# One row of the output projection moved from the last load of a decode kernel to its first

## The chip, the cores and the metric

The kernel runs on one core of one Trainium2 chip. The metric is device time in microseconds of one execution. In the profile PE is TensorE (PEld its weight loads), DVE is VectorE, ACT is ScalarE, POOL is GpSimd and SP is SyncE.

## The reference

One token passes through a layer with two parallel branches, attention over a sliding window of cached keys and values, and a small MLP:

```
xn  = layernorm(x)                                # x: 1 x 1024
q   = xn @ wq                                     # wq: 1024 x 4096, 32 heads of 128
k,v = last W = 4096 positions of the caches       # 4 kv heads, each for 8 query heads
p   = softmax(q k^T / sqrt(128));  o = p v
A   = o @ wo                                      # wo: 4096 x 1024
B   = gelu(layernorm(xn) @ w1 + b1) @ w2 + b2     # w1: 1024 x 3584, w2: 3584 x 1024
out = x + A + B                                   # 1 x 1024, bf16
```

All inputs are bf16. Nearly all bytes are read once: wq and wo 8 MB each, w1 and w2 7 MB each, 4 MB of K and 4 MB of V.

## The kernel before, in words

Four large buffers in SBUF, `slot0` to `slot3`, each 128 partitions by 16384 bf16, are reused in turn. Every large load goes through SP's queue, one after another, in the order in which SP issues it. A load into a slot that is still being read is issued only when the readers are done, so SP waits at these places.

The order of loads is: wq's first row and K's four heads (before a barrier of all engines at L203), then wq's other rows in three loads, b1 and b2, w1 in two loads, V, w2 in three loads, and wo in seven. "Row" c of wq, wo, w1 and w2 is what one matmul step takes: a tile of 128 partitions, one weight row on each partition; the view is `"(p c) n -> p c n"`. wo has 32 such rows (`CWO`), each 128 x 1024 bf16, 256 KB, of 2 KB per partition. Rows 0 to 15 go into `slot0` in two loads of eight rows. Rows 16 to 31 go into `slot2` in five loads, cut at

```
cuts = [0, 8, 12, 14, 15, 16]
```

so that the last two loads hold one row each, 30 and 31. A load is the unit that is waited for: each has a semaphore of its own, and `wo_row(c)` gives the tile and the key of the load that row c came with.

The work is written as a list of operations with the names that they read and write. The class `Plan` works out from it which operation waits for which; each engine then carries out its own in the order of the list.

VectorE transposes K (L334, four steps) and copies it into order (L343, shared with ScalarE, L339). TensorE multiplies by wq meanwhile. Scores, softmax, V and the MLP's first half follow. VectorE sums 21 of w2's 28 rows, each scaled by its activation, in f32 (`run[0]`, `run[1]`; L479 and L482) and adds the two sums in L518. TensorE does the other seven (`PE_ROWS`) and wo's rows 0 to 23 (`NB` is 24) into `sc_ps` as `bulk`. VectorE then adds `bulk` to `run[0]` (L550, in two halves).

The end of the kernel is the loop over wo's rows 24 to 31. Each row is four matmuls into the two banks of `acc2` (`acc_a` 288 columns wide, `acc_b` 224), with the two halves of the output at partitions 0 and 32. After row 27 eight f32 matmuls (L233 in the profile) fold `run[0]` into the same accumulators. L227 is the helper `mm` in which all the single-row matmuls are recorded, L219 the helper `ldw` for their weights, and L213 the helper `dma`. VectorE (L569) and ScalarE (L570) cast the two banks to bf16, and SP and ScalarE store the halves.

The loads ahead of the barrier are issued at L194 (K) and L199 (wq's first row, and x on ScalarE's queue). The plan learns of them by entries that issue nothing and only name the semaphore, such as

```
plan.add("sp", lambda: None, (), ("wq0",), wq_sem)
```

Of the kernel before, what the change touches and what calls it, by code (L numbers as in the profile page):

```python
# [8 lines left out]
BF16 = mybir.dt.bfloat16  # L9
# [123 lines left out]
def kernel(  # L133
# [14 lines left out]
    nc = tc.nc  # L148
    P = 128
    D = A_x.shape[-1]  # L150
    Hkv = A_k_cache.shape[1]
    Sk = A_k_cache.shape[2]
    Dh = A_k_cache.shape[3]
    NQ = A_wq.shape[1]
    Hq = NQ // Dh
# [8 lines left out]
    CWO = NQ // P  # L164
    NA = 288
    NB = 24
# [7 lines left out]
    def sb(name, shape, dt):  # L174
        return nc.alloc_sbuf_tensor(name, shape, dt).ap()

    def ps(name, shape):
        return nc.alloc_psum_tensor(name, shape, FP32).ap()

    slot = [sb(f"slot{i}", [P, 16384], BF16) for i in range(4)]  # L180
    kT = sb("kT", [P, 4, 4, W // 4], BF16)
    acc2 = ps("acc2", [P, 2, 512])
# [4 lines left out]
    x_flat = A_x.rearrange("a b d -> (a b d)")  # L187
    k_sb, kt_scr = slot[0], slot[3]
    k_sem = [nc.alloc_semaphore(f"k{g}") for g in range(Hkv)]
    wq_v = A_wq.rearrange("(p c) n -> p c n", p=P)  # L190
    wq_sem = nc.alloc_semaphore("wq0")

    def load_k(g):
        return nc.sync.dma_start(out=k_sb[g:P - Hkv + g + 1:Hkv, :],  # L194
                                 in_=A_k_cache[0, g, Sk - W:Sk, :].rearrange("(r c) d -> r (c d)", r=P // Hkv))

    x32 = sb("x32", [Hq, Hq], BF16)
    x_sem = nc.alloc_semaphore("x32")
    for i, sem in [(nc.sync.dma_start(out=slot[1][:, 0:NQ], in_=wq_v[:, 0, :]), wq_sem)] + [(load_k(g), k_sem[g]) for g in range(Hkv)] + [(nc.scalar.dma_start(out=x32, in_=x_flat.rearrange("(a j) -> a j", a=Hq)), x_sem)]:  # L199
        i.then_inc(sem, 16)  # L200
        tc.no_tile_sem_insts.add(i.ins.name)
    tc.close()
# [2 lines left out]
    plan = Plan(nc)  # L205
    pe, dve, act, pool, sp = nc.tensor, nc.vector, nc.scalar, nc.gpsimd, nc.sync

    def op(eng, fn, r=(), w=()):
        plan.add(eng, fn, r, w)

    def dma(eng, out_ap, in_ap, r=(), w=(), over=()):
        q = plan.engines[eng]
        plan.add(eng, lambda: q.dma_start(out=out_ap, in_=in_ap), r, w, True, over)  # L213

    def ldw(w_ap, pos, r):
        def go():
            with nc.discard():
                i = pe.ldweights(w_ap, tile_position=pos).ins
            return pe.add_instruction(mybir.InstLdweights(  # L219
                name=nc.get_next_instruction_name(), engine=i.engine, tile_size=(P, 32), tile_position=pos, ins=i.ins, outs=i.outs))  # L220
        op("pe", go, r, ())

    def mm(out_ap, w_ap, x_ap, start, stop, pos, r, w):
        def go():
            with nc.discard():
                i = pe.matmul(out_ap, lhsT=w_ap, rhs=x_ap, start=start, stop=stop, tile_position=pos).ins
            return pe.add_instruction(mybir.InstMatmult(  # L227
                name=nc.get_next_instruction_name(), engine=i.engine, start_tensor_calc=start, stop_tensor_calc=stop,
                tile_size=i.tile_size, tile_position=i.tile_position, ins=i.ins, outs=i.outs, ldweights=False))
        op("pe", go, r, w)  # L230

    def mm32(out_ap, w_ap, x_ap, start, stop, r, w, pos=None):
        op("pe", lambda: pe.matmul(out_ap, lhsT=w_ap, rhs=x_ap, start=start, stop=stop, tile_position=pos), r, w)  # L233

    plan.add("sp", lambda: None, (), ("wq0",), wq_sem)
    for g in range(Hkv):
        plan.add("sp", lambda: None, (), (f"k{g}",), k_sem[g])
# [1 line left out]

    w1_v = B_w1.rearrange("(p c) n -> p c n", p=P)  # L240
    w2_v = B_w2.rearrange("(p c) n -> p c n", p=P)
    wo_v = A_wo.rearrange("(p c) n -> p c n", p=P)
    wq_t = [slot[1 + i].rearrange("p (r n) -> p r n", r=4) for i in range(2)]
    wq_cuts = ((0, 1, 2), (0, 2, 4), (1, 0, 4))
    for i, a, b in wq_cuts:
# [91 lines left out]
    for s0, s1 in ((0, 1), (1, 2), (2, 4)):  # L337
        for (R, Cd) in pairs[:ACT_PAIRS]:
            op("act", lambda s0=s0, s1=s1, R=R, Cd=Cd: act.copy(out=kT[32 * Cd:32 * Cd + 32, R, s0:s1, :].rearrange("p s (c j) -> p (s c) j", j=32),  # L339
                                                                in_=T3[32 * R:32 * R + 32, 32 * s0:32 * s1, Cd, :]), [f"scr{s}" for s in range(s0, s1)], (f"kTa{R}{Cd}{s0}",))  # L340
    kt_keys = [f"kTa{R}{Cd}{s}" for (R, Cd) in pairs[:ACT_PAIRS] for s in range(3)]
    for n, (R, Cd) in enumerate(pairs[ACT_PAIRS:]):
        op("dve", lambda R=R, Cd=Cd: dve.tensor_copy(out=kT[32 * Cd:32 * Cd + 32, R, :, :].rearrange("p s (c j) -> p (s c) j", j=32),  # L343
                                                     in_=T3[32 * R:32 * R + 32, :, Cd, :]), [f"scr{s}" for s in range(NS)], (f"kTd{R}{Cd}",))
# [32 lines left out]
    for c in (2, 3):  # L377
        for t in range(4):
            ldw(xw[:, 96 + P * c:97 + P * c], (0, 32 * t), ("xw",))
        for b in range(2):  # L380
            for t in range(4):
                j = 2 * (3 - t) + b
# [121 lines left out]
    wo_t = [slot[s].rearrange("p (r n) -> p r n", r=16) for s in (0, 2)]  # L504
    for a in (0, 8):
        dma("sp", wo_t[0][:, a:a + 8, :], wo_v[:, a:a + 8, :], (), (f"wo0{a}",), ("slot0",))
    cuts = [0, 8, 12, 14, 15, 16]
    for a, b in zip(cuts[:-1], cuts[1:]):
        dma("sp", wo_t[1][:, a:b, :], wo_v[:, 16 + a:16 + b, :], (), (f"wo1{a}",), ("slot2",))
    o_m = sb("o_m", [Hq, Hkv, Dh], FP32)  # L510
# [26 lines left out]
    o8 = sb("o8", [P, 32], BF16)  # L537
# [2 lines left out]
    bulk_rows(PE_ROWS, w2_row, hcol, "hT", first=True)  # L540

    def wo_row(c):
        i, r = divmod(c, 16)
        return wo_t[i][:, r, :], f"wo0{r // 8 * 8}" if i == 0 else f"wo1{max(a for a in cuts if a <= r)}"

    ocol = lambda c: o8[:, c:c + 1]
    bulk_rows(list(range(16)), wo_row, ocol, "o8")
    bulk_rows(list(range(16, NB)), wo_row, ocol, "o8", last=True, groups=2)
    for half in range(2):
        op("dve", lambda half=half: dve.tensor_tensor(out=run[0][0:33, 512 * half:512 * half + 512], in0=bulk[:, half, :],  # L550
                                                      in1=run[0][0:33, 512 * half:512 * half + 512], op=ALU.add), ("bulk", "run0"), (f"sum{half}",))
    acc_a, acc_b = acc2[:, 0, 0:NA], acc2[:, 1, 0:512 - NA]
    parts = [(acc_a, 0, NA, "acc_a"), (acc_b, NA, 512, "acc_b")]
    for c in range(NB, CWO):
        wap, key = wo_row(c)
        for half in range(2):
            ldw(o8[:, c:c + 1], (0, 32 * half), ("o8",))
        for acc, a, b, akey in parts:
            for half in range(2):
                pr, h0 = 32 * half, 512 * half  # L560
                mm(acc[pr:pr + 1, :], o8[:, c:c + 1], wap[:, h0 + a:h0 + b], c == NB, c == CWO - 1, (0, pr), (key,), (akey, "acc2"))
        if c == NB + 3:
            for acc, a, b, akey in parts:
                for half in range(2):
                    pr, h0 = 32 * half, 512 * half
                    mm32(acc[pr:pr + 1, :], ones_f[:, 0:1], run[0][:, h0 + a:h0 + b], False, False,
                         ("ones_f", "run0", f"sum{half}"), (akey, "acc2"), (0, pr))
# [37 lines left out]
```

## Time and profile before

| | |
|---|---|
| time, median of 3 runs | 100.66 us (100.49 to 100.67) |
| time of the profiled execution | 100.62 us |
| its span | 98.80 us |
| mean granted TensorE clock | 0.896 |
| bytes read | 39.86 MB, 403 GB/s over the span |
| K's last load landed | 15.56 us |
| wo's rows 16 to 23, first matmul | 91.47 us |
| wo's rows 24 to 27, first matmul | 93.95 us |
| last matmul row, start | 96.53 us |

Times in the views are microseconds from the start of the span of the profiled execution; that execution's time is 1.82 us longer than its span. In a line of the order of time the two first numbers are start and length, `x16` is the number of instructions that were merged, and what stands in brackets is how long the engine sat idle before the first of them and what ended that. In the chain of waits each piece is the work, the transfer or the engine's own issue that the next piece waited for.

### The profile page before, as it was taken

To read this page: it belongs to the slowest core of one execution; us is meant where nothing else is said; L and a number is where in the kernel's file an instruction comes from. 1 tells how busy PE (TensorE), PEld (TensorE's weight loads), DVE (VectorE), ACT (ScalarE), POOL (GpSimd) and SP (SyncE) were. 2 spreads that over 40 slices of the span, in tenths; PEclk is the share of its full clock that TensorE was granted. 3 is DMA by queue.
4 is the path that set the end of the run, shared out by engine and by line. 5 is a ranking of instruction groups with operands and counts; after the bars stand their busy time and mean duration, and the time that the engine had idled before them with its cause. 6 is when DMAs were issued, how large, how long until landed. Compare 5 with 4: busy or idle time off the path is not lost.

```text
span 98.8 us, 961 instructions
## 1 busy us (share of the span) xinstructions
PE 57.2 (58%) x323; PEld 16.2 (16%) x220; DVE 73.9 (75%) x75; ACT 30.7 (31%) x29; POOL 10.0 (10%) x22
## 2 busy tenths in 40 slices
PE   0032040598200699960899586667670999594792
PEld 0022000123000233410202121212210111110130
DVE  0023776999999999999102677899999999999431
ACT  0050000089999899992001075100000000000001
POOL 0072580000000680000000000000000000000000
PEclk9999999999985556997558999999999589999999
DMA  3999979999999999999799999999998999999970
GB/s 50 448 418 451 464 328 458 441 511 438 424 424 405 395 453 453 395 441 464 338 424 424 418 441 413 463 424 429 487 418 383 431 431 424 424 424 405 405 265 1
DMA packets 3132, 39.86 MB, mean 403 GB/s; under 512 B 438, under 2 KB 444, under 8 KB 828
## 3 DMA queue, kind: packets, MB, share of 16 engines
q1 hardware_dynamic: 3082, 39.86, 95.4%
q10 hardware_dynamic: 50, 0.00, 0.0%
HBM read 39.86 MB, written 0.00 MB: 403 GB/s over the span
## 4 chain that ended last, share of the span: by engine, by line
DVE 36%; DMA 32%; PE 20%; issue 5%; SPq 2%; ACT 2%; DVEq 0%
DMA slot<-in_A_wo_dram 20%; DVE slot L334 18%; DVE kT L343 13%; DMA slot<-in_A_k_cache_dram 13%; PE qo_ps L495 10%; PE sc_ps L227 6%; PE acc L227 2%; SPq L194 2%; ACT e L450 1%; DVE eTb L454 1%; DVE m_loc L435 1%; PE acc L233 1%; DVE q_sb L388 1%; ACT sc L427 1%; DVE res L569 0%
## 5 line engine op out<-in xcount | busy, mean ns | idle before, releaser
L339 ACT COPY kT<-slot 32x1024 bf16<-32x1024 bf16 (+1 forms) x18 | 23.9, 1327 | 14.3 <-DVE slot L334 14.1
L482 DVE SCALAR_TENSOR_TENSOR run<-slot,hTf,run 128x1024 f32<-128x1024 bf16 x20 | 24.2, 1272 | 0.0
L369 PE MATMUL acc<-slot,xw 128*128 x48 | 15.7, 494 | 12.6 <-DMA slot<-in_A_wq_dram 12.2
L334 DVE STREAM_TRANSPOSE slot<-slot 128x4096 bf16<-128x4096 bf16 x4 | 17.4, 4414 | 1.2 <-DMA slot<-in_A_k_cache_dram 1.2
L343 DVE COPY kT<-slot 32x4096 bf16<-32x4096 bf16 x10 | 13.2, 1316 | 0.2
L495 PE MATMUL qo_ps<-slot,eTb 128*128 (+1 forms) x32 | 10.2, 382 | 5.1 <-issue 4.0
L227 PE MATMUL sc_ps<-slot,o 128*1 128x512 bf16 x48 | 9.1, 378 | 2.8 <-DMA slot<-in_A_wo_dram 2.8
L369 PEld LDWEIGHTS acc<-slot,xw 128*128 x48 | 5.5, 115 | 23.5 <-issue 21.1
L570 ACT CAST res<-acc 33x224 bf16<-33x224 f32 x1 | 0.3, 338 | 20.1 <-PE acc L227 20.1
L227 PE MATMUL sc_ps<-kT,qm 128*32 128x512 bf16 x32 | 6.1, 973 | 0.3 <-DVE qm L416 0.3
L495 PEld LDWEIGHTS qo_ps<-slot,eTb 128*128 (+1 forms) x32 | 3.1, 96 | 12.0 <-issue 8.7
L428 DVE COPY sc<-sc_ps 128x512 f32<-128x512 f32 x1 | 0.7, 691 | 5.7 <-PE sc_ps L227 5.7
L227 PE MATMUL sc_ps<-slot,hT 128*1 128x512 bf16 x14 | 4.7, 509 | 0.1
L538 ACT CAST o<-misc 128x32 bf16<-128x32 f32 x1 | 0.2, 186 | 14.6 <-PE misc L233 14.6
L219 PEld LDWEIGHTS <-o 128*1 128x1 bf16 x40 | 2.4, 83 | 12.4 <-issue 11.8
L233 PE MATMUL misc<-x,spread 32*128 32x8 bf16 x4 | 0.3, 168 | 6.2 <-POOL spread L255 6.2
L249 DVE MEMSET mhalf<- 128x1 f32 x1 | 0.1, 59 | 5.0 <-PEq L203 5.0
L233 PE MATMUL acc<-spread,qm 32*128 32x512 bf16 x4 | 1.6, 498 | 3.7 <-POOL qm L315 3.7
L227 PE MATMUL acc<-slot,yT 128*1 128x448 bf16 x64 | 3.4, 353 | 0.0
L427 ACT COPY sc<-sc_ps 128x512 f32<-128x512 f32 x1 | 0.6, 585 | 8.8 <-PE sc_ps L227 8.8
L251 ACT ACT_TABLE_LOAD x1 | 1.3, 1283 | 4.8 <-PEq L203 4.8
L227 PE MATMUL acc<-slot,o 128*1 128x288 bf16 (+1 forms) x32 | 2.2, 272 | 0.6 <-DMA slot<-in_A_wo_dram 0.6
(88 smaller groups left out, 46.0 us busy)
## 6 DMA issues: line engine op xcount, KB each, us to landing
slot<-in_B_w_dram SPq DMA_DIRECT2D x3, 3584.0 KB, 16.6
slot<-in_A_wo_dram SPq DMA_DIRECT2D x3, 2048.0 KB, 22.8
slot<-in_A_k_cache_dram SPq DMA_DIRECT2D x4, 1024.0 KB, 9.8
slot<-in_A_wq_dram SPq DMA_DIRECT2D x1, 4096.0 KB, 27.0
slot<-in_A_v_cache_dram SPq DMA_DIRECT2D x1, 4096.0 KB, 16.1
slot<-in_A_wq_dram SPq DMA_DIRECT2D x2, 1024.0 KB, 9.2
slot<-in_A_wq_dram SPq DMA_DIRECT2D x1, 2048.0 KB, 17.8
slot<-in_B_w_dram SPq DMA_DIRECT2D x1, 2048.0 KB, 21.5
```

What stands on the lines that cost most here:

```text
L194: return nc.sync.dma_start(out=k_sb[g:P - Hkv + g + 1:Hkv, :], in_=A_k_cache[0, g, Sk - W:Sk, :].rearrange("(r c) d -> r (c d)", r=P // Hkv))
L219: return pe.add_instruction(mybir.InstLdweights(name=nc.get_next_instruction_name(), engine=i.engine, tile_size=(P, 32), tile_position=pos ...
L227: return pe.add_instruction(mybir.InstMatmult(name=nc.get_next_instruction_name(), engine=i.engine, start_tensor_calc=start, stop_tensor_c ...
L233: op("pe", lambda: pe.matmul(out_ap, lhsT=w_ap, rhs=x_ap, start=start, stop=stop, tile_position=pos), r, w)
L251: op("act", lambda: act.activation(out=dummy[:, 0:1], in_=mhalf[0:1, 0:1], func=ACT.Exp), ("mhalf",), ("act_warm",))
L334: op("dve", lambda s=s: dve.transpose(out=scr[:, s, :], in_=k2[:, s, :]), ("k0", "k1", "k2", "k3", "slot0"), (f"scr{s}",))
L339: op("act", lambda s0=s0, s1=s1, R=R, Cd=Cd: act.copy(out=kT[32 * Cd:32 * Cd + 32, R, s0:s1, :].rearrange("p s (c j) -> p (s c) j", j=32), ...
L343: op("dve", lambda R=R, Cd=Cd: dve.tensor_copy(out=kT[32 * Cd:32 * Cd + 32, R, :, :].rearrange("p s (c j) -> p (s c) j", j=32), in_=T3[32 ...
L369: pe.matmul(acc2[:, b, :], lhsT=xw[:, bass.ds(32 * n + 512 * i, P)], rhs=slot[1 + i][:, bass.ds(1024 * n + 512 * b, 512)], start=False, st ...
L427: op("act", lambda: act.copy(out=sc[:, 512:1024], in_=sc_ps[:, 1, :]), ("sc1",), ("scs1",))
L482: op("dve", lambda: dve.scalar_tensor_tensor(out=t, in0=wap, scalar=hTf[:, c:c + 1], in1=t, op0=ALU.mult, op1=ALU.add), (key, "hTf", f"run ...
L495: return pe.matmul(qo_ps, lhsT=cols, rhs=v4[:, :, c, :], start=first, stop=last)
```

## The change

wo's row 31 gets a tile of its own, `wo_last`, and its load is issued first of all, ahead of wq's first row and K. The last load of wo goes: `cuts` ends at 15, so row 30's load is now the last one to be issued before the output. `wo_row(31)` gives the new tile and key. The last loop takes row 31 first and then rows 24 to 30; the f32 matmuls still come after row 27. The number of matmuls, of loads and of bytes is the same.

```diff
-    wq_sem = nc.alloc_semaphore("wq0")
+    wq_sem, wo_sem = nc.alloc_semaphore("wq0"), nc.alloc_semaphore("wo_last")
+    wo_v = A_wo.rearrange("(p c) n -> p c n", p=P)
+    wo_last = sb("wo_last", [P, D], BF16)
...
-    for i, sem in [(nc.sync.dma_start(out=slot[1][:, 0:NQ], in_=wq_v[:, 0, :]), wq_sem)] + [(load_k(g), k_sem[g]) for g in range(Hkv)] + [(nc.scalar.dma_start(out=x32, in_=x_flat.rearrange("(a j) -> a j", a=Hq)), x_sem)]:
+    first = [(nc.sync.dma_start(out=wo_last, in_=wo_v[:, CWO - 1, :]), wo_sem), (nc.sync.dma_start(out=slot[1][:, 0:NQ], in_=wq_v[:, 0, :]), wq_sem)]
+    for i, sem in first + [(load_k(g), k_sem[g]) for g in range(Hkv)] + [(nc.scalar.dma_start(out=x32, in_=x_flat.rearrange("(a j) -> a j", a=Hq)), x_sem)]:
...
+    plan.add("sp", lambda: None, (), ("wo_last",), wo_sem)
     plan.add("sp", lambda: None, (), ("wq0",), wq_sem)
...
-    wo_v = A_wo.rearrange("(p c) n -> p c n", p=P)
...
-    cuts = [0, 8, 12, 14, 15, 16]
+    cuts = [0, 8, 12, 14, 15]
...
     def wo_row(c):
+        if c == CWO - 1:
+            return wo_last, "wo_last"
...
-    for c in range(NB, CWO):
+    tail = [CWO - 1] + list(range(NB, CWO - 1))
+    for c in tail:
...
-                mm(acc[pr:pr + 1, :], o8[:, c:c + 1], wap[:, h0 + a:h0 + b], c == NB, c == CWO - 1, (0, pr), (key,), (akey, "acc2"))
+                mm(acc[pr:pr + 1, :], o8[:, c:c + 1], wap[:, h0 + a:h0 + b], c == tail[0], c == tail[-1], (0, pr), (key,), (akey, "acc2"))
```

## The prediction

> **What bounds the kernel now.** I began with the first two parts of the page, then the chain of waits, then the order of time at both ends of the span, where the change sits. The page:
>
> ```profile
> span 98.8 us, 961 instructions
> PE 57.2 (58%) x323; PEld 16.2 (16%) x220; DVE 73.9 (75%) x75; ACT 30.7 (31%) x29; POOL 10.0 (10%) x22
> DMA  3999979999999999999799999999998999999970
> ```
>
> The transfers are busy in nearly every slice, 39.86 MB in one stream. VectorE, at 75%, is the second candidate. The chain that ended last says which of the two sets the end:
>
> ```profile
> 74.51 19.40 DMA slot<-in_A_wo_dram
> 93.91 0.04 issue
> 93.95 1.03 PE acc L227 x14
> 94.99 0.86 PE acc L233 x6
> 95.85 0.66 PE acc L227 x11
> 96.51 0.02 issue
> 96.53 0.30 PE acc L227 x2
> 96.83 0.02 issue
> 96.86 0.45 DVE res L569
> ```
>
> From 74.51 to 93.91 the chain is the landing of wo's rows 24 to 27; then TensorE works to 96.83, then the casts and the store. The order of time from 91 us shows the slack beside it:
>
> ```profile
> 90.71 1.23 DVE L518 TENSOR_TENSOR run<-run 128x1024 f32<-128x1024 f32 x1
> 91.47 1.89 PE L227 MATMUL sc_ps<-slot,o 128*1 128x512 bf16 x16 [1.29 <-DMA slot<-in_A_wo_dram]
> 93.39 1.28 DVE L550 TENSOR_TENSOR run<-sc_ps,run 33x512 f32<-33x512 f32 x2 [1.46 <-PE sc_ps L227]
> 93.95 1.03 PE L227 MATMUL acc<-slot,o 128*1 128x288 bf16 x16 [0.60 <-DMA slot<-in_A_wo_dram]
> 94.83 1.03 PE L233 MATMUL acc<-run,ones_f 128*1 128x288 f32 x8
> 95.69 1.22 PE L227 MATMUL acc<-slot,o 128*1 128x288 bf16 x16
> ```
>
> TensorE starts rows 16 to 23 when they land (91.47), idles 0.60 before rows 24 to 27 land, and from 93.95 has unbroken work: four rows, the eight f32 matmuls that fold `run[0]` in, four rows. VectorE waited 1.46 us before L550, so its long row sum is not on the path.
>
> Is the last stretch TensorE's pace, or the landing of row 31? Two narrow windows of TensorE's order of time, at 96.32 to 96.40 and 96.56 to 96.64, and the last load as it stands in the issues:
>
> ```profile
> 96.12 0.38 PE L227 MATMUL acc<-slot,o 128*1 128x288 bf16 x4
> ...
> 96.53 0.28 PE L227 MATMUL acc<-slot,o 128*1 128x288 bf16 x2
> ```
>
> ```profile
> 75.93 0.43 SPq L213 DMA_DIRECT2D slot<-in_A_wo_dram  x1
> ...
> slot<-in_A_wo_dram SPq DMA_DIRECT2D x1, 256.0 KB, 20.6
> ```
>
> Rows 28, 29 and 30 start at 95.69, 95.91 and 96.12, so one row costs 0.22 us of issue. Row 31 should have started at 96.34; it starts at 96.53, and its load, issued at 75.93, landed 20.6 us later, at 96.53. So **row 31 is waited for by 0.19 us**, and the two limits, transfers and TensorE's tail, lie only that far apart.
>
> **The change, part by part.**
>
> *Row 31 leaves the end of the queue.* TensorE's last part after the f32 matmuls is now rows 28, 29, 30. Row 31 goes ahead of row 24, into TensorE's idle 0.60 us, and costs 0.22 there with 0.38 left over: nothing on the path. On the path one row goes, -0.22, and so does the wait for it, -0.19, if nothing else is late. Together -0.41.
>
> *Row 31 goes ahead of everything.* The 256 KB are now in front of wq, K and all other loads, so each of these lands later by the time that the row takes; call that s. The row waits for wo that TensorE leaves at 81.67, 86.57 and 91.47 are 4.90 us apart for 2 MB each: 256 KB take 0.61 at that pace. The tail with its short packets is slower: rows 24 to 27 land at 93.93 and row 31, 1 MB later, at 96.53, which is 2.60 or 0.65 a row. Row 31's packets are 2 KB each wherever it stands, so I take s = 0.65, and 0.61 as the nearest lower value.
>
> *What the lateness s does.* K's last load lands at 15.56 and VectorE's transposes start at once (15.58, after 1.18 idle), so VectorE's whole chain moves by s: L518 ends at 91.94 + 0.65 = 92.59. L550 needs TensorE's rows 16 to 23, which land s later too and end at 93.39 + 0.65 = 94.04; the slack of 1.46 stays, as both move alike. Rows 24 to 27 start at 93.95 + 0.65 = 94.60, the f32 matmuls at 95.48, row 28 at 96.34, row 29 at 96.56, row 30 at 96.77.
>
> *The last landing.* The sum of bytes in front of the last one is unchanged, so row 30 lands where row 31 did, at about 96.53: TensorE comes to it at 96.77, 0.24 later. What ends last is then TensorE's tail, not the transfer. Against row 31's start at 96.53 the end moves by s - 0.41 = 0.65 - 0.41 = **+0.24 us**.
>
> *What costs nothing.* SP issues one more load before the barrier at L203 and one fewer at the end (the seven of wo, from 58.77, become six). An issue with its gap is 0.46 us (0.80 to 1.26). Moved past it at the start are wq's first row, K's four, and behind the barrier wq's other three and b1, b2; also all engines' first work, since they leave the barrier after SP's last K issue. The layernorm work on VectorE ends at 14.41, so 14.87 then, before K at 16.2; TensorE's zeroing of `acc2` ends at 13.8, and its first wq rows start only at 18.36. If that cover were gone, the price would be the 0.46. The stream does not run dry anywhere: w1's second half is issued by 33.36 while the first lands at 41.2, V at 43.57 with w1 landing at about 49.6, the third wo load at 74.14 with wo's rows 8 to 15 landing at 86.5. Row 31's wait on its own semaphore is met long before TensorE gets there at 94.
>
> *The unknown: what the first 256 KB cost at a cold start.* These slices are the trace's start; the last two columns are the transfer share and GB/s:
>
> ```profile
> 1.80:2.00 0.20, 0.00 (x0) 0.00 (x0) 0.00 (x0) 0.00 (x0) 0.00 (x0) 1.00 2.08 328
> 2.20:2.40 0.20, 0.00 (x0) 0.00 (x0) 0.00 (x0) 0.00 (x0) 0.00 (x0) 1.00 0.27 41
> 2.60:2.80 0.20, 0.00 (x0) 0.00 (x0) 0.00 (x0) 0.00 (x0) 0.00 (x0) 1.00 0.80 248
> 3.20:3.40 0.20, 0.00 (x0) 0.00 (x0) 0.00 (x0) 0.00 (x0) 0.00 (x0) 1.00 1.39 575
> ```
>
> First bytes come at 1.8, a microsecond after the issue, and from 1.8 to 3.2 the seven slices sum to 0.30 MB, where the later pace (2 MB in 4.90 us) would give 0.60: a loss of 0.69 us. The first eight packets, 8 KB each, take 2.08 x 16 x 0.20 / 8 = 0.83 us each. If the loss is the same whatever goes first, s stays 0.65. If short packets pay it instead of wq's, s can fall as far as 0.65 - 0.69, about nothing. If short packets pay it and wq's then pay half of it again, s is 0.65 + 0.34 = 0.99. I take 0.65: the row at the tail is the same transfer, and a loss of latency per engine is paid once.
>
> **The rivals.**
>
> *The cold start swallows row 31 (faster).* The 0.69 us of slow start falls on row 31 in place of wq's first row, so K lands where it did. For it: the slow slices are there, and row 31's 256 KB are about the 0.30 MB that they carried. Against it: by 3.2 us before also had 0.30 MB moved, so the same bytes by then means no gain; only a per-packet loss gives one, and SP issues wq 0.46 later. At s = 0 the gain is 0.41: 100.25 us by the median. It decides faster from s below 0.21.
>
> *A tie.* With s between 0.21 and 0.61 the end moves by less than 0.2 us; s = 0.46, the issue alone, gives +0.05, 100.71. For it: 0.61 is the steady pace, already at the edge.
>
> *The start pays twice (slower by more).* The transfer engines finish their shares of row 31 before wq's packets have come, or wq's packets are slow again. Against it: row 31 is 0.6 us of work and wq is issued only 0.46 behind. At s = 0.99 it gives +0.58, 101.24.
>
> *A load alone pays its whole latency (slower by much).* The first load before, wq's row of 1 MB, landed 5.1 us after its issue, of which its bytes take 2.45: 2.65 us are latency at its two ends. If the stream behind row 31 started only once that row had landed, at 0.80 + 2.65 + 0.65 = 4.1, the stream would be 2.3 us later than its first bytes at 1.8: s = 2.3, an end 1.9 later, 102.55. Against it: at the tail, row 31 landed about 0.65 behind row 30, with nothing of a latency between them, and K's four loads, issued 0.6 apart, land at a steady 2.4 us a MB. The Trainium skill, "DMA: Bandwidth & Descriptors", section Anatomy of one DMA, has a rule of this kind that speaks against small loads: about 2 us fixed for each, beside its bytes at 436 GB/s, fitted on another issue path. An estimate from that page is 2.6 us for this load alone, against the 0.65 that the tail's rows take here in a full queue.
>
> **How the numbers follow.** The profiled execution took 100.62 us, 1.82 outside its span; the forecast for it is 100.86. It lies 0.04 below the median of 100.66, so the forecast is 100.66 + 0.24 = 100.90. A measurement of this kernel can tell about 0.2%, 0.20 us. Chances: forecast, s from 0.61 to 0.85, 0.40; the start pays twice, 0.09; the whole latency, 0.03; tie, 0.35; cold start swallows the row, 0.13. Slower is 0.40 + 0.09 + 0.03 = 0.52. The range leaves out most of the swallowed start and the whole latency: from 100.50 (s = 0.25) to 101.35 (s = 1.10).
>
> **What would show it.** Right: K's transposes start 0.6 to 0.7 later, at about 16.2; wo's rows 16 to 23 start on TensorE at 92.1; row 31's matmuls stand in the gap before row 24; rows 28 to 30 run at 0.22 us each without a wait, and row 30 starts near 96.77. Wrong: transposes at 15.6 and an end before 96.8 (swallowed); row 30 waiting for its landing; K later than 16.5 (paid twice).

## The result, and the profile after

The changed kernel took 101.90 us (median of 6 executions, 100.99 to 102.64), the kernel before 100.61; the ratio is 1.0118 (95% interval 1.0077 to 1.0159). Compared again it was 101.50 (101.01 to 102.99) and 1.0070 (1.0025 to 1.0115). So it is slower, by more than forecast, and it scatters. Three of the first six executions also had 2.6 to 3.1 us outside the span in place of 1.8, and 14 of 105 executions of the kernel before have 2.3 to 3.4 there; I therefore compare spans: 99.7 us in the median of 15 executions (99.1 to 100.4) against 98.7 (98.5 to 99.4). That is **+1.0 us** where +0.24 was forecast.

The profiled execution, with a span of 99.2 us, is among the fastest of the fifteen. Its page:

```profile
span 99.2 us, 961 instructions
PE 59.2 (60%) x323; PEld 16.4 (17%) x220; DVE 74.0 (75%) x75; ACT 30.8 (31%) x29; POOL 10.0 (10%) x22
DMA  2999998999999999998999999999897999999950
```

The end of its chain of waits:

```profile
75.12 19.56 DMA slot<-in_A_wo_dram
94.68 0.04 issue
94.72 1.03 PE acc L230 x16
95.76 0.86 PE acc L236 x7
96.62 0.58 PE acc L230 x10
97.20 0.02 issue
97.22 0.45 DVE res L575
```

The same stretch of its order of time, with the start of the transposes (lines have moved by 3 to 6):

```profile
16.36 8.77 DVE L337 STREAM_TRANSPOSE slot<-slot 128x4096 bf16<-128x4096 bf16 x2 [1.51 <-DMA slot<-in_A_k_cache_dram]
...
92.23 1.89 PE L230 MATMUL sc_ps<-slot,o 128*1 128x512 bf16 x16 [1.29 <-DMA slot<-in_A_wo_dram]
...
93.95 0.38 PE L230 MATMUL acc<-wo_last,o 128*1 128x288 bf16 x4
...
94.72 1.03 PE L230 MATMUL acc<-slot,o 128*1 128x288 bf16 x16 [0.39 <-DMA slot<-in_A_wo_dram]
...
95.59 1.03 PE L236 MATMUL acc<-run,ones_f 128*1 128x288 f32 x8
...
96.46 0.82 PE L230 MATMUL acc<-slot,o 128*1 128x288 bf16 x12
```

Row 31 (`wo_last`) runs in the gap, and the last three rows run without the pause that stood at 96.53 before: that part is as forecast. The transposes start at 16.36 against 15.58, so s is 0.78, and the cast starts at 97.22 against 96.86, +0.36, which is s - 0.41. Only s is larger than the 0.65 I took. In the profile of the second comparison it is larger still: transposes at 16.74, s = 1.16, cast at 97.60, +0.74, again s - 0.41.

```profile
16.74 4.45 DVE L337 STREAM_TRANSPOSE slot<-slot 128x4096 bf16<-128x4096 bf16 x1 [1.90 <-DMA slot<-in_A_k_cache_dram]
...
97.60 0.45 DVE L575 CAST res<-acc 33x288 bf16<-33x288 f32 x1 [1.78 <-PE acc L230]
```

Both values are measured against a profile that is itself a little late at this place: K's last share landed at 15.56 there, and at 15.21 to 15.29 in three kernels below with the same head (row31_after_k, row31_late, before_cuts).

What s is made of shows at the end of the stream. These are windows of the kernel before, then of the changed kernel in the second comparison; the last two columns are the transfer share and GB/s:

```profile
95.40:95.80 0.40, 0.40 (x8) 0.09 (x2) 0.00 (x0) 0.00 (x0) 0.00 (x0) 1.00 0.49 174
95.80:96.20 0.40, 0.40 (x12) 0.17 (x4) 0.00 (x0) 0.00 (x0) 0.00 (x0) 1.00 0.06 20
```

```profile
95.40:95.80 0.40, 0.40 (x12) 0.17 (x4) 0.40 (x1) 0.00 (x0) 0.00 (x0) 1.00 0.35 128
95.80:96.20 0.40, 0.40 (x10) 0.17 (x4) 0.02 (x1) 0.00 (x0) 0.00 (x0) 1.00 0.15 56
96.20:96.60 0.40, 0.40 (x6) 0.17 (x4) 0.00 (x0) 0.00 (x0) 0.00 (x0) 1.00 0.06 20
```

Between 95.4 and 95.8 fewer engines are left at work in the changed kernel than before, and yet some work 0.4 us longer: the sixteen transfer engines are out of step. The trace has one semaphore increment for each engine's share of a load. Of row 30's sixteen, thirteen come by 96.11 and three at 96.46, 96.68 and 96.94. The same pattern is there at K's first load: thirteen by 8.43, three at 8.96, 9.18 and 9.44; before, all sixteen came from 7.62 to 8.25, and as far apart, 0.63, at the end. A lag of the start is thus still there at the end of a stream that is busy in nearly every slice, and each load lands with the slowest share. The Trainium skill says in "DMA: Bandwidth & Descriptors", section Why a DMA increments its semaphore by 16 and not by 1, that the engines finish independently and only the full count means that all has landed; the trace agrees, down to the 0.83 us between the thirteenth and the last.

Where the three fell behind can be read from the packets of the same trace. The one that comes last lost its time on wq's first row: fifteen shares of that row land by 5.90 and one at 6.99, as a single 8 KB packet took 1.48 us (from 5.19 to 6.67) in place of 0.31; two packets of K's later (6.99 + 2 x 1.22 = 9.43) that engine fits the share at 9.44. The other two began K late, at 5.79 and 5.93, with packets of 1.62 and 1.68 us in place of 1.21. In the first profile one engine alone began K late, at 6.18 where the others had begun by 5.77, and its packets ran at 1.33 and 1.21. All this happens as K's turn comes, between 5.2 and 7.6.

### The profile page after: what moved, and what is told of

Same layout as the page of the kernel before. It is cut to its first block, busy times and chain, and to the rows that moved or that the text cites. A ratio compares the mean times of both kernels' runs of the same rounds, so it can differ in the third digit from the quotient of the medians.

```text
span 99.2 us, 961 instructions
## 1 busy us (share of the span) xinstructions
PE 59.2 (60%) x323; PEld 16.4 (17%) x220; DVE 74.0 (75%) x75; ACT 30.8 (31%) x29; POOL 10.0 (10%) x22
## 4 chain that ended last, share of the span: by engine, by line
DMA 64%; PE 24%; issue 4%; SPq 1%; DVE 0%
DMA slot<-in_A_wq_dram 27%; DMA slot<-in_A_wo_dram 20%; DMA slot<-in_A_v_cache_dram 17%; PE qo_ps L498 12%; PE acc L372 10%; PE acc L230 2%; PE acc L236 1%; SPq L216 1%; DVE res L575 0%
## 5 line engine op out<-in xcount | busy, mean ns | idle before, releaser
L498 PE MATMUL qo_ps<-slot,eTb 128*128 (+1 forms) x32 | 11.5, 434 | 4.1 <-issue 2.6
L230 PE MATMUL sc_ps<-slot,hT 128*1 128x512 bf16 x14 | 5.9, 609 | 0.5 <-DMA slot<-in_B_w_dram 0.5
L230 PE MATMUL sc_ps<-kT,qm 128*32 128x512 bf16 x32 | 5.6, 902 | 0.3 <-DVE qm L419 0.3
```

Of the source, the lines that this page charges most:

```text
L230: return pe.add_instruction(mybir.InstMatmult(name=nc.get_next_instruction_name(), engine=i.engine, start_tensor_calc=start, stop_tensor_c ...
L498: return pe.matmul(qo_ps, lhsT=cols, rhs=v4[:, :, c, :], start=first, stop=last)
```

## The experiments

The numbers, then each in turn. "Over before" is the median span less that of the kernel before in the same comparison; the ratio is of times. Where row 31 is moved, 0.2 to 0.3 of it are the row's own bytes, as the second and third line show. The diffs are shortened, with words in place of calls.

| kernel | executions | median span, us | over before | ratio (95%) |
|---|---|---|---|---|
| again | 9 | 99.7 | 1.0 | 1.0070 (1.0025 to 1.0115) |
| row31_after_k | 12 | 98.9 | 0.2 | 1.0032 (1.0004 to 1.0060) |
| row31_late | 12 | 99.0 | 0.3 | 1.0024 (0.9998 to 1.0050) |
| split_wq | 6 | 99.95 | 1.25 | 1.0128 (1.0096 to 1.0161) |
| row31_second | 10 | 99.45 | 0.65 | 1.0060 (1.0035 to 1.0086) |
| split_rev | 7 | 100.0 | 1.2 | 1.0113 (1.0082 to 1.0143) |
| split_k3_later | 4 | 100.05 | 1.25 | 1.0125 (1.0062 to 1.0188) |
| row31_act | 10 | 99.4 | 0.6 | 1.0052 (1.0005 to 1.0099) |
| k_issue_late | 4 | 99.75 | 1.15 | 1.0127 (1.0090 to 1.0164) |
| split4 | 4 | 99.8 | 1.2 | 1.0113 (1.0082 to 1.0143) |
| wq2_first | 10 | 98.7 | 0.1 | 1.0024 (0.9988 to 1.0061) |
| k0_first | 6 | 99.1 | 0.5 | 1.0050 (1.0029 to 1.0072) |
| row31_wq2 | 10 | 98.8 | 0.1 | 1.0006 (0.9978 to 1.0035) |
| k_issue_later | 10 | 99.65 | 0.95 | 1.0099 (1.0060 to 1.0138) |
| k0_alone | 3 of 4 | 100.3 | 1.6 | 1.0160 (1.0089 to 1.0230) |
| row31_wq2_cuts | 12 | 99.1 | 0.5 | 1.0047 (1.0027 to 1.0066) |
| before_cuts | 12 | 98.85 | 0.25 | 1.0047 (1.0014 to 1.0079) |

### Is it the head or the tail?

**again**, the changed kernel with no edit.

> The changed kernel once more, for the spread of its times. Its profiled execution took 100.99 us and moved by s - 0.41 with s = 0.78 (transposes at 16.36 in place of 15.58), which is +0.37; its other five runs took 101.47 to 102.64. Theory 'head': the slow start of the transfers at the front of the stream differs from run to run when a load of 2 KB a partition goes first, so s differs: spans from 99.1 to 100.1 and times from 100.9 to 102.6 come again. Theory 'tail': the excess comes from the tile of its own or from the order in TensorE's last loop: the same times, but the transposes start at 16.2 to 16.4 whatever the time. Theory 'chance': the spread was of that chip, and all times now lie within 0.3 of 101.0.

The scatter came back, with s as told above: "head".

**row31_after_k** and **row31_late**: the same tile and the same last loop, row 31 loaded later.

```diff
-    first = [(row 31), (wq row 0)]; then K's four
+    first = [(wq row 0)]; then K's four, then (row 31)        # row31_after_k
...
+    dma("sp", wo_last, wo_v[:, CWO - 1, :], (), ("wo_last",))  # row31_late, ahead of wo's rows 0 to 7
```

> Row 31 into its own tile as in the change, its load issued behind K's four instead of ahead of wq's first row; TensorE's last loop as in the change. K lands as before (transposes at 15.6), wo's rows 16 to 30 still land one row's 0.61 to 0.65 later. Theory 'head': what was over the 0.61 to 0.65 is gone, and so is the spread: +0.20 to +0.24, 100.8 to 100.9, runs within 0.3. Theory 'tail': the tile and the loop are those of the change, so times up to 102.6 as there. A third, that K's lateness through VectorE's chain is what counts: equal to the kernel before or 0.2 faster.

> Row 31 into its own tile, its load issued just ahead of wo's rows 0 to 7, when the queue is full; the head is the kernel before's, TensorE's last loop that of the change. Theory 'head': s = 0.61 to 0.65 for rows 0 to 30 of wo only: +0.20 to +0.24, 100.8 to 100.9, runs within 0.3. Theory 'tail': 101.0 to 102.6 as the change. Third, K's chain: equal or faster.

+0.2 and +0.3 of span, and a range of 0.4 and 0.5 in place of 1.3. In row31_late the chain of waits ends:

```profile
94.45 1.03 PE acc L230 x16
95.49 0.86 PE acc L236 x8
96.35 0.58 PE acc L230 x10
96.93 0.02 issue
96.95 0.45 DVE res L575
```

Rows 24 to 27 start 0.50 later than before (93.95), TensorE's tail is unbroken, and the cast is +0.09. The forecast of +0.24 describes these two kernels. It is the head that makes the change different.

**split_wq**: the kernel before, with wq's first row in two loads; no byte changes its place.

```diff
-    load(wq row 0)
+    load(wq row 0, columns 0 to 1023); load(wq row 0, columns 1024 to 4095)
```

> The kernel before, with wq's first row in two loads, its first 1024 columns (256 KB, 2 KB a partition, as row 31 is) and the other 3072 behind them; the order of all bytes and TensorE's last loop are the kernel before's. It has the small first load and one issue more at the head alone. Theory 'head': K lands 0.1 to 0.2 later (0.78 less the 0.61 to 0.65 of the bytes), and as the stream ends later by as much or more from run to run, 100.8 to 102, with the change's spread. Theory 'tail': equal to the kernel before, 100.6, within 0.2.

The loss is 1.25 with no row moved, more than I expected for K's landing: transposes at 16.61.

```profile
1.72 2.49 SPq L194 DMA_DIRECT2D slot<-in_A_k_cache_dram  x4
...
16.61 4.45 DVE L335 STREAM_TRANSPOSE slot<-slot 128x4096 bf16<-128x4096 bf16 x1 [1.71 <-DMA slot<-in_A_k_cache_dram]
```

The bytes that the change puts in front are not needed for it.

### What in the head?

**row31_second** and **split_rev** put the large load first; **split_k3_later** takes the barrier back to its old place; **row31_act** takes row 31 out of SP's queue.

```diff
+    first = [(wq row 0), (row 31)]                             # row31_second
+    load(wq row 0, 0 to 3071); load(wq row 0, 3072 to 4095)    # split_rev
+    split_wq, with K's fourth load issued behind the barrier   # split_k3_later
+    nc.scalar.dma_start(out=wo_last, ...)                      # row31_act, in place of nc.sync
```

> The change with the two first loads swapped: wq's first row (1 MB), then row 31 (256 KB), then K. K's first load is the third of the queue as in the change, and the same bytes stand ahead of it. Known so far: K's second and later loads keep their pace, and what is lost is lost before K's first load ends. Theory 'small first': the small load is drained before the next load reaches all transfer engines, so what counts is that it goes first; then nothing is lost here: transposes at 15.9 to 16.2, span +0.2 to +0.3 over the kernel before (98.9 to 99.0). Theory 'third load': a load that is third in the queue reaches some transfer engines only 4 us after its issue; same bytes ahead, same place, so a loss as in the change: spans 99.2 to 100.0. Theory 'barrier': K's first packets start at or after the end of the barrier at 5.2 and are held up there: also 99.2 to 100.0.

> wq's first row in two loads again, now the 3072 columns (768 KB) first and the 1024 (256 KB) second; bytes, order of all else and number of loads as in the split with the small one first, which cost 1.2 us of span. Theory 'small first': no loss, span 98.6 to 98.8. Theory 'third load' and theory 'barrier': K's first load is again third and starts about 5.2, span 99.8 to 100.0.

> The split with the small load first, but K's fourth load is issued behind the barrier instead of ahead of it, so SP has five loads ahead of it as in the kernel before and the barrier ends at 4.75. Order of the queue unchanged. Theory 'barrier': the loss of 1.2 us goes, span 98.6 to 98.9. Theory 'third load' and theory 'small first': the loss stays, span 99.8 to 100.0.

> The change, but row 31's load is issued on ScalarE's queue (ahead of x), at the same time as SP issues wq's first row; wq's and K's issues, and the barrier, are then as in the kernel before. Theory 'third load' and theory 'barrier': the loss goes and only the bytes stay, span +0.2 to +0.3 (98.9 to 99.0). Theory 'small first': also +0.2 to +0.3, since wq's load is in its own queue at once; if what costs is only that a small cold load stands there at all, 99.2 to 100.0 as in the change.

"Small first" falls: split_rev loses as much as split_wq. "Barrier" falls: in split_k3_later the barrier was over at 4.55, earlier than in the kernel before, and the loss stayed; in row31_after_k it ended at 5.13 and nothing was lost. "Third load" is left, but row31_act speaks against it: wq and K were issued as in the kernel before and its span is 0.6 longer, 0.3 to 0.4 more than the row's bytes ask for. There the two queues share the engines: wq's row landed at 6.81 against 5.87, and its shares were spread over 1.09 us against 0.68; the slow packets are wq's and row 31's, from 3.7 to 4.5, and K's run at 1.21 to 1.26. The Trainium skill, "Trainium Kernel Development and Optimization", section Key Constraints, says that issuing from several engines only saves issue time, since the transfers run on the same engines and interleave. The issue time was saved here and some time was still lost; why the shares drift apart is open.

### The issue of K's first load

**k_issue_late** adds no load at all: SP only waits, for a memset of GpSimd's on a scratch tile, before it issues K.

```diff
+    hold, hold_sem = sb("hold", [P, 900], FP32), nc.alloc_semaphore("hold")
+    nc.gpsimd.memset(hold, 0.0).then_inc(hold_sem, 1)
+    nc.sync.wait_ge(hold_sem, 1)                               # between wq's row and K
```

> The kernel before, with K's first load issued about 0.45 us later (SP waits for a memset of GpSimd's, on a scratch tile, that nothing else reads) and nothing added to the queue: wq's row first, K second. The theory 'small first' has fallen (the split with the large part first lost as much), so has 'barrier'. Theory 'issue': K's first load reaches all transfer engines at full pace only 3.5 to 4 us after its issue, in the kernel before just in time for the end of wq's first row; then this loses 0.4 to 1.2 us: span 99.1 to 99.9 and K's first load landing spread out over 1 us as in the splits. Theory 'count': a third load at the head is slow because two others are being taken apart ahead of it; then nothing is lost here: span 98.5 to 98.8.

This is the clearest run. SP's queue and the transposes:

```profile
0.80 0.40 SPq L199 DMA_DIRECT2D slot<-in_A_wq_dram  x1
1.67 2.43 SPq L194 DMA_DIRECT2D slot<-in_A_k_cache_dram  x4
...
16.31 8.77 DVE L341 STREAM_TRANSPOSE slot<-slot 128x4096 bf16<-128x4096 bf16 x2 [2.41 <-DMA slot<-in_A_k_cache_dram]
```

K is issued at 1.67 in place of 1.26, with wq's 1 MB (2.5 us at the later pace) still ahead of it, and lands 0.73 later; the median span grows by 1.15, as theory 'issue' had it. In the windows of the stretch in which K's first load starts, the kernel before comes first, then this one:

```profile
4.40:6.80 2.40, 0.26 (x4) 0.18 (x4) 0.49 (x4) 1.49 (x2) 1.64 (x5) 1.00 1.23 529
```

```profile
4.40:6.80 2.40, 0.22 (x4) 0.18 (x4) 0.22 (x2) 1.49 (x2) 1.30 (x3) 1.00 1.11 358
```

The engines are nearly as busy (1.11 against 1.23) for two thirds of the bytes: K's first packets run slowly. In the trace, a 32 KB packet takes 1.21 us in the kernel before; here the first one of each engine takes 1.3 to 2.2, and the shares of K's first load land from 7.95 to 8.26 on six engines and from 8.57 to 8.95 on ten. The turn of a load, below, is the start of its first packet: 4.80 for K's first load in the kernel before, 4.66 here.

**split4**, **wq2_first** and **k0_first** vary what stands ahead of K.

```diff
+    load(wq row 0) in four loads of 1024 columns, then K       # split4
+    load(wq row 0); load(wq row 1); then K                     # wq2_first
+    load(K 0); load(wq row 0); load(K 1) ...                   # k0_first
```

> wq's first row in four loads of 256 KB ahead of K; all bytes and their order as in the kernel before. K's first load is the fifth, issued at 2.6 in place of 1.26. Theory 'issue': its full pace comes at 6.1 to 6.6 in place of 4.8, so the loss grows from the 1.2 of the split in two to 1.6 to 2.2: span 100.3 to 101.0. Theory 'count': the loss grows with each load, by 0.6 to 1.2 for each of two more: span 101 to 102.3. If only the presence of one more load counts, span 99.9 as the split in two.

> wq's first two rows (1 MB each) ahead of K, so that K's first load is third and issued at 1.72, but 2 MB stand ahead of it, which last until about 7.2 us. Bytes in all as in the kernel before; K lands 2.4 us later, and VectorE's slack ahead of L550 is 1.46, so about 1.0 of that shows at the end of the span; the transfers are read by the last load's landing instead (96.49 in the kernel before). Theory 'issue' and theory 'count' with cover: last landing at 96.3 to 96.6, no loss. If a third load is slow whatever is ahead of it, 97.0 to 97.6.

> K's first load ahead of wq's first row; all bytes the same. It shows how long K's load takes to its first bytes when nothing is ahead. Theory 'issue': its first packets start 3 us or more after the issue at 0.8, or run far below their pace until 4.5, and the whole stream ends 0.5 to 2 us later: span 99.3 to 101. Theory 'count': first packets at 1.8 as wq's row, no loss, span 98.5 to 98.9.

In wq2_first K is issued as late as in the change (1.72), but 2 MB stand ahead of it; its packets start at 7.1 and all but three take 1.21; the shares land within 0.40 us, the last load at 96.38, and nothing is lost. That K came 2.05 us later (transposes at 17.63) cost nothing either, where I had expected 1.0.

```profile
1.72 2.43 SPq L194 DMA_DIRECT2D slot<-in_A_k_cache_dram  x4
...
17.63 17.42 DVE L336 STREAM_TRANSPOSE slot<-slot 128x4096 bf16<-128x4096 bf16 x4 [2.79 <-DMA slot<-in_A_k_cache_dram]
```

In k0_first, with nothing ahead, K's first packets start at 2.15 on eight engines and take 1.85 to 2.2 us, and at 2.85 on the other eight: the slow start is K's own, seen without cover. It cost 0.5, between the two forecasts. In split4 the loss did not grow, against both theories and as the last alternative had it; there nearly all of K's packets run at 1.21, and the time is lost among the small loads of wq ahead of it: 2 KB packets slow from 4.1 to 4.6, the shares of the last two loads 1.04 and 1.10 us apart. With the slow 8 KB packet of the change's second profile this says that slow packets are not a matter of K's 32 KB rows alone.

### The size of the loss, and the cover given back

> Row 31 first as in the change, but with wq's first two rows ahead of K in place of one: K's first load is fourth and issued at 2.2, but 2.25 MB stand ahead of it, so its turn comes at about 7.7. Theory 'lead': no loss is left, only the row's own 0.61 to 0.65: span +0.2 to +0.3 over the kernel before (98.8 to 99.0), the last load landing at 96.3 to 96.6 and TensorE's row 30 behind it. If a small first load costs something by itself: 99.2 to 100.0 as the change.

**row31_wq2** is the change with wq's first two rows ahead of K (and `wq_cuts` without row 1):

```diff
-    first = [(row 31), (wq row 0)]
+    first = [(row 31), (wq row 0), (wq row 1)]
```

The loss is gone: +0.1 of span, ratio 1.0006, even a little less than forecast. The end of its chain:

```profile
94.28 1.03 PE acc L230 x13
95.31 0.86 PE acc L236 x8
96.17 0.58 PE acc L230 x9
96.75 0.02 issue
96.77 0.45 DVE res L576
```

Row 30 landed at 96.14, its shares within 0.35 us, and TensorE came to it at 96.44: TensorE's tail ends last, as forecast.

**k_issue_later** is k_issue_late with a memset twice as long (K issued at 2.46); **k0_alone** issues K's other loads only after VectorE's `xc`.

> As the kernel whose K was issued 0.4 us late, with about 0.8 more: K's first load issued at about 2.5, its turn at 4.7 as before, so a lead of 2.2 in place of 3.0 (and 3.5 in the kernel before). Theory 'lead': the loss grows by about the 0.8: span 100.4 to 100.7. If it is a fixed penalty for coming too late, span 99.6 to 100.0 again.

> As the kernel whose K was issued 0.4 us late, but K's other three loads are issued only when VectorE has centred x (about 6 us), so SP issues nothing between 2.3 and 6. It is read by the packets of K's first load (32 KB each, 1.21 us at the steady pace, 1.3 to 2.2 in the late kernel between 4.7 and 6.5). Theory 'lead': they are as slow as there, and the span is as long or longer, 99.6 to 101. Theory 'issuing': they run at 1.21 to 1.3, as nothing is being issued beside them.

0.8 us later costs no more: 0.95 against 1.15. Thirteen shares of K's first load land by 7.92, three at 8.74 to 8.86, and three packets took 1.9 to 2.0. So it is a fixed loss of about 0.8 us on some engines, not the delay handed on. In k0_alone, with nothing being issued from 2.3 to 6.4, K's first packets still took up to 2.1, so "issuing" falls; K's second load, issued at 6.46 with its turn at about 7.7, began with six packets of 1.9 to 2.1. This profile is of the longest of its four executions, 102.2, where one share of the second load came 2.6 us behind the others; the table has the other three, 100.0 to 100.9.

**row31_wq2_cuts** and **before_cuts**: `cuts = [0, 4, 8, 10, 12, 14, 15]`, and the same with 16 at its end.

> Row 31 first and two rows of wq ahead of K, and wo's rows 16 to 27 in loads of 4, 4, 2 and 2 rows in place of 8 and 4, so that TensorE can do rows 16 to 19, 24 and 25 while it waited before. If TensorE's tail ends last there, as its last row at 96.44 with a landing at 96.14 says, row 30 now starts at its landing, 96.15 to 96.3: span 98.4 to 98.7, 0.1 to 0.4 below the kernel without these cuts, and 0 to 0.3 below the kernel before. If the landings end last, or the two more loads cost the stream their own time, 98.7 to 99.0.

> The kernel before with the same finer loads. Its end is row 31's landing at 96.49, with TensorE 0.19 us early, so nothing is won: span 98.6 to 98.9. If TensorE's tail were what ends last there, it would win 0.2 to 0.4.

Neither wins (99.1 lies above both forecasts for the first, 98.85 within that for the second), and no kernel of this study beats the kernel before. In before_cuts row 31 still starts at its landing, after a longer wait:

```profile
96.38 0.38 PE L227 MATMUL acc<-slot,o 128*1 128x288 bf16 x4 [0.25 <-DMA slot<-in_A_wo_dram]
```

In row31_wq2_cuts the profiled execution had lost step again, one engine of wq's second row by 0.57 us, and row 30 landed at 96.83. Its head is that of row31_wq2, so the cover does not keep every execution in step; with it wq's second row stands where K's first load stands in the change, third in the queue and issued at 1.72. Whether TensorE's tail would win there with the engines in step was not seen.

## Why the prediction was wrong

- **What bounds the end**: right. Transfers and TensorE's tail lie 0.2 us apart, and the second ends last with row 31 ahead (row 30 at 96.89 with its landing at 96.57; row31_wq2 likewise).
- **The tail's -0.41**: right to 0.02 in both profiles of the change. Two readings under it were a little late, rows 24 to 27 landing at 93.91 and row 31 at 96.49 rather than 93.93 and 96.53; 2.58 us for four rows is still 0.65 a row.
- **The lateness s = 0.65**: the term that was mis-sized. It was 0.78 and 1.16 in the two profiles, and +1.0 of span asks for about 1.4 in the median. Placed later in the queue, the same row gave spans of +0.2 and +0.3, as forecast, so the bytes were sized well.
- **"What costs nothing"**: this is the step that failed. I named SP's one more issue, 0.46 us, and hid it behind a queue that does not run dry, at a price of 0.46 if the cover were gone. The queue did not run dry of loads, and yet, with K's first load issued at 1.72 in place of 1.26, one to three transfer engines fell behind by 0.4 to 1.1 us as its turn came, and every later load waited for them. k_issue_late shows the price of the later issue with neither row nor load: about 1.1 us for 0.41 of delay. row31_after_k, where the row's issue stands behind K's, loses none of it, and wq2_first and row31_wq2 show the cover that was needed, 2 MB ahead of K in place of 1.25.
- **The cold start of the first 256 KB**: I looked for the unknown in the wrong load. From 1.8 to 3.2 us the changed kernel moved more than the kernel before, 294 GB/s against 218; the loss came at K's turn, after 4.4.
- **The rivals**: "the start pays twice" was nearest in place and size (+0.58, 101.24), with 0.09. It had wq's packets slow again, and in the second profile one of them is what the last share waits for; the other late engines lost their time on K's first packets, which it did not have. I set it aside since wq is issued only 0.46 behind. The swallowed start and the tie did not happen, and the whole latency (+1.9) was too much. The range ended at 101.35 because I priced a lost start by its mean over the engines; the landings take the slowest.
- **K's lateness through VectorE**: right that it is covered; 2.05 us of it cost nothing.

Open: why the engines fall behind. What orders the kernels is when K's first load is issued and what is ahead of it. With 1 or 1.25 MB ahead, those that issue it at 1.67 or later all lose, and those that issue it at 1.26 do not, but for row31_act; with 2 MB or more ahead, an issue at 1.72 (wq2_first) or 2.19 (row31_wq2) loses nothing, though row31_wq2_cuts lost some on wq's second row. The time from issue to turn is not the measure by itself: it is 3.4 to 3.5 in the kernel before and the others without loss, and 3.0 and 2.5 in the late ones with it, but 3.6 in row31_second, and 3.7 and 3.6 in the two profiles of the change, which lose with a longer wait than the kernel before has. The number of loads ahead is not either: k_issue_late has one, as the kernel before, and loses; wq2_first has two and does not. Whether the two act together, no run shows. Which engines fall behind, the records do not say.

## What to carry to other kernels

A kernel whose transfers never idle pays at its end for what a single transfer engine loses at its start, since each load waits for the slowest of its sixteen shares: look at the spread of a load's semaphore increments, not only at the mean rate. Price one more issue at the head by whose issue it delays, and try more bytes ahead of that load: here 2 MB ahead of K gave the loss back in two kernels, 1.25 MB did not. Moving a load forward makes all that it passes late by its bytes, so a row taken off the tail must save more than it delays; here it saved 0.41 against some 0.61 for its bytes at the stream's pace, and the best kernel with it measured +0.1.

## What the runs showed of the hardware that I had not expected

K's 32 KB packets take 1.21 us at the steady pace; in k_issue_late the first on each of the sixteen engines took 1.3 to 2.2, in k_issue_later three took 1.9 to 2.0. The lag then stayed to the last load: in the change's second profile three engines late by 0.53 to 1.01 at 9 us against the thirteenth at 8.43, and by 0.35 to 0.83 at 96. With row 31 on a second queue at the head the span was 0.6 us longer, 0.2 to 0.3 of it the row's bytes, even with wq and K issued as early as before.
